# Attention with pooled keys and a gated convolution layer, one core: the order of a whole kernel's instructions from a new table, the first keys projected once, the last units gated on TensorE

## The chip, the cores and the metric

The kernel runs on one core of one Trainium2 chip. The metric is the device time of one execution in microseconds. The names of the engines in the profile: PE is TensorE (PEld its weight loads), DVE is VectorE, ACT is ScalarE, POOL is GpSimd, SP is SyncE, whose queue issues every DMA.

## The reference

```python
kv_pool = kv.reshape(B, H//4, 4, W//4, 4, C).mean(axis=(2, 4))      # B=4, 384x32 pixels, C=128
k = v = kv_pool.reshape(B, -1, C) @ w_sr                            # 768 keys per batch
s = (q @ k.transpose(0, 2, 1)) / sqrt(C)                            # 12288 queries per batch
a = exp(s - s.max(-1)); a /= a.sum(-1) + 1e-9
x = a @ v
gate = sigmoid(sum over 5 taps of conv_w[k] * x shifted by 4-k rows) # causal, per channel
out = (gate * (x @ w_val)) @ w_out
```

q is drawn 8 times and conv_w 200 times larger than in the plain layer, so the products keep float32's accuracy by splitting operands into a high and a low part.

## The kernel before, in words

The work is cut into groups of 512 queries (four tiles of 128), 24 groups per batch, 96 in all; the last group is two units of 256 (`LAST = (2, 2)`). A tile goes through these steps (`group`, L488):

- `score`: six matmuls into a PSUM tile `s` of 768 columns (high keys by high q, low keys by high q, high keys by low q). There are three `s` tiles.
- `row_max` (DVE, `nm`), `expo` (ACT), `unit_over_z` (two short DVE steps, `r`), then the high half `hl` (ACT, L579) and the low half (DVE, L590). Only this last DVE step gives the `s` tile back.
- `turn`: a transposing DMA of two tiles at once, `pt<-hl` (SP, L603). So a group needs two of them.
- 18 matmuls `av<-pt,vh` or `vl` (L674) once both are there, then `x` (ACT), the five-tap convolution on POOL (L731, L739; on DVE, L713 and L715, for the last three units, `TAIL`), `th` (tanh, ACT), `val` (PE, L756), `h` (DVE), `out` (PE, L765), `evac` (ACT, L770), and a store.

Per batch `setup` (L267) makes the keys and values: 16 pieces of kv are loaded (`kvt`, 384 KB each, L283), each is summed over 16 pixels (DVE, L305, in two halves; for some pieces of the first batch on POOL, L324), and the sums are projected by `w_sr` (PE, L359), split into `kh`, `kl` and `vt` (ACT L375, L387, DVE L399) and turned to values (L452 to L473). The first batch is set up before anything else can run; batches 2 to 4 are loaded two pieces at a time during the groups of the batch before, in eight blocks each, 20 us apart.

The order of all instructions is made by `Plan.order`: each step carries a duration, a due time from the table `DUE`, and the steps and buffers that it waits for; the planner walks through a model of the engines and takes on each the ready step with the earliest due time. The engines then run their lists strictly in that order. `WAIT`, `CLUMP` and `PERIOD` are weights of the same planner, `FIRST_Q` and `FIRST_VALS` its times for the first loads of q and the first values.

In the first batch the projection is cut by piece (17 parts, `project`, L346). `AGAIN = 3` issues each of the first 14 parts three times into the same place (L358); the repeats change no result. The eleven parts of the first 512 keys go to bank `m`, the rest to `av`:

```python
for _ in range(n):
    nc.tensor.matmul(steps[0].tile[:, c0 - lo:c1 - lo], wsr,
                     st["pool"][:, c0:c1], start=True, stop=True)
...
steps.append(part(c0, c1, AGAIN if first and c1 <= NK - 3 * PC else 1))
```

Of the kernel before, what the change touches and what calls it, by code (L numbers as in the profile page):

```python
# [22 lines left out]
PERIOD = 10.01  # L23
DUE = dict(keys=-40.3, vals=-31.67, vals0=8.05, q=-55.06, qh=7.59, ql=-74.93,
           score=(-7.35, -6.03, -4.51, -6.24), max=(-15.0, -3.7, 0.12, -12.81),
           exp=(5.62, -26.1, -4.96, -12.51), hi=(-28.69, -23.8, -4.13, -31.54),
           lo=(21.73, -24.19, 6.06, 6.76), turn=(-4.97, 24.57, 24.86, -0.88), pe=4.52, thi=58.42,
           tlo=9.94, r=(-46.22, -49.7, -33.31, -24.78), grid=-0.79, av=20.59, avs=4.62,
           halo=63.02, x=44.45, gate=28.59, th=59.85, val=49.41, h=2.48, out=18.96, evac=16.49,
           store=49.37)  # L30
# [11 lines left out]
class Plan:  # L42
# [5 lines left out]
    WAIT = dict(PE=0.08, ACT=0.3, DVE=0.1, POOL=0.01, SP=0.27)  # L48
    DMA_LEAD, DMA_TAIL, CLUMP = 1.3, 0.8, 24.47
# [99 lines left out]
def attn_moe_kernel(ctx, tc, qT, kvT, w_sr, w_moe, outT):  # L149
# [14 lines left out]
    D = DUE  # L164
# [67 lines left out]
    def weights():  # L232

        load_sr = plan.add("SP", 0.3, -20 * T - 35.5, lambda: nc.sync.dma_start(out=wsr, in_=w_sr))
# [32 lines left out]
    def setup(b, st):  # L267
# [7 lines left out]
        def load(i):  # L275
            buf = "o" if first and i in SPARE else "kvt"
            cuts = (0, PC * RR // 2, PC * RR) if first and i == PIECES - 1 else (0, PC * RR)

            def run(k):
                if k == 0:  # L280
                    steps[0].tile = tile_of(steps[0], buf)
                sl = slice(cuts[k], cuts[k + 1])
                nc.sync.dma_start(out=steps[0].tile[:, sl], in_=kvT[b, i, :, sl])  # L283
            steps = []
            for k in range(len(cuts) - 1):
                steps.append(plan.add(
                    "SP", (1.0 if first else 1.3) / (len(cuts) - 1),
                    due(-20 * T + i) if first else at(i), lambda k=k: run(k), steps[:],
                    takes=(buf,) if k == 0 else (), start=at(i)))
            return steps, buf  # L290
# [7 lines left out]
        def summed(i, ld, buf, part):  # L298
# [3 lines left out]
            def run():  # L302
                dst = pool_of(s, k0)[:, k0:k0 + n]
                src = ld[0].tile[:, :PC * RR].rearrange("c (k s) -> c k s", s=RR)
# [3 lines left out]
                         [ld[min(part, len(ld) - 1)], sums.get(0)], takes=("pool",) if k0 == 0 else (),  # L308
                         frees=[(ld[0], buf)], start=at(i))
# [542 lines left out]
```

## Time and profile before

| | |
|---|---|
| median of 3 runs | 1037.87 us (1037.05 to 1038.72) |
| the profiled execution | 1038.03 us, span 1036.2 us, so 1.83 us lie outside the span |
| PE busy | 1001.3 us, 97% of the span |
| DVE, POOL, ACT busy | 931.0, 928.8, 882.3 us (90%, 90%, 85%) |
| chain of waits | PE 81%, DMA 5%, DVE 4% |

The span runs from the first to the last instruction. A busy engine is one with an instruction in it, which for PE includes the repeated projections. The table of slices of the page shows PE below nine tenths in the first three slices only, and in the last.

### The profile page before, as it was taken

The page shows a single profiled execution, that of the slowest core. Times are in us where ns is not written, and L with a number is a line of the kernel's source. Part 1 is how long each engine was busy: PE and PEld are TensorE (multiplying, and loading weights), DVE is VectorE, ACT ScalarE, POOL GpSimd, SP SyncE. Part 2 cuts the span into 40 slices and gives each one's busy share as a digit, 9 for nine tenths or more (in the row PEclk, how much of TensorE's full clock was granted, in tenths as well). Part 3 has the DMA queues.
Part 4 walks back from the last instruction along what each step waited for, and adds up shares of the span by engine and source line. Part 5 has one row for each costly group of instructions (what it writes and reads, how often), then busy time and mean ns, then how long its engine had stood idle before and what let it go on. Part 6 is the DMA issues. An engine that isn't in the chain of part 4 may idle for free.

```text
span 1036.2 us, 15524 instructions
## 1 busy us (share of the span) xinstructions
PE 1001.3 (97%) x4600; PEld 618.6 (60%) x4600; DVE 931.0 (90%) x1810; ACT 882.3 (85%) x1575; POOL 928.8 (90%) x1067
## 2 busy tenths in 40 slices
PE   5779999999999999999999999999999999999997
PEld 5656655556665555566665565556666666666664
DVE  5699999999899999998989898999998898988985
ACT  0588998889898898899998898889999999889884
POOL 4159999999999998999999899899999999999994
PEclk9899999999999999999999999999999999999999
DMA  8399999999999999999999999999999999999983
GB/s 316 84 206 257 226 239 243 253 218 201 220 223 233 246 232 254 237 248 239 184 220 237 240 237 245 245 239 219 182 225 205 212 218 218 202 211 192 192 176 91
DMA packets 616851, 227.06 MB, mean 219 GB/s; under 512 B 595520, under 2 KB 596160, under 8 KB 616768
## 3 DMA queue, kind: packets, MB, share of 16 engines
q1 hardware_dynamic: 616768, 226.07, 101.1%
q8 instruction: 37, 0.61, 0.3%
q14 instruction: 46, 0.38, 0.1%
HBM read 50.66 MB, written 25.17 MB: 73 GB/s over the span
## 4 chain that ended last, share of the span: by engine, by line
PE 81%; DMA 5%; DVE 4%; ACT 1%; issue 1%; SPq 0%; ACTq 0%; DVEq 0%
PE s L532 34%; PE av L674 31%; PE m L765 7%; PE m L756 7%; DMA pt<-hl 3%; DMA kvt<-in_kv 2%; DVE hl L590 2%; DVE nm L544 1%; ACT hl L579 1%; DVE h L760 0%; PE m L452 0%; DVE pool L305 0%; PE m L359 0%; SPq L603 0%; ACT s L551 0%
## 5 line engine op out<-in xcount | busy, mean ns | idle before, releaser
L739 POOL TENSOR_TENSOR gate<-gate,tap 128x512 f32<-128x512 f32 x376 | 480.6, 1278 | 9.9
L590 DVE SCALAR_TENSOR_TENSOR hl<-s,r,hl 128x768 f16<-128x768 f32 x382 | 386.4, 1012 | 39.8 <-ACT hl L579 39.6
L674 PE MATMUL av<-pt,vh 128*128 128x512 f16 (+1 forms) x1164 | 384.3, 379 | 2.4 <-DMA pt<-hl 1.8
L551 ACT ACTIVATE s<-s,nm 128x768 f32<-128x768 f32 x384 | 336.4, 876 | 51.3 <-DVE nm L544 50.8
L544 DVE TENSOR_REDUCE nm<-s 128x1 f32<-128x768 f32 x384 | 362.5, 944 | 9.6 <-PE s L532 8.9
L579 ACT ACTIVATE hl<-s,r 128x768 f16<-128x768 f32 x382 | 338.4, 906 | 31.7 <-DVE r L565 24.0
L532 PE MATMUL s<-kh,qh 128*128 128x512 f32 (+1 forms) x768 | 265.7, 427 | 16.4 <-DVE hl L590 8.8
L731 POOL TENSOR_SCALAR tap<-x,wb 128x512 f32<-128x512 f32 x376 | 253.4, 693 | 0.0
L674 PE MATMUL av<-pt,vl 128*128 128x512 f16 (+1 forms) x582 | 219.6, 377 | 0.0
L532 PEld LDWEIGHTS s<-kh,qh 128*128 128x128 f32 x768 | 136.0, 191 | 128.5 <-issue 47.3
L674 PEld LDWEIGHTS <-vh 128*128 128x128 f16 x1164 | 112.3, 98 | 153.6 <-issue 56.4
L532 PE MATMUL s<-kl,qh 128*128 128x512 f32 (+1 forms) x768 | 199.9, 342 | 0.0
L532 PE MATMUL s<-kh,ql 128*128 128x512 f32 (+1 forms) x768 | 198.6, 340 | 0.0
L518 POOL TENSOR_TENSOR ql<-q,qh 128x512 fp32r<-128x512 f32 (+1 forms) x97 | 122.7, 1266 | 31.1 <-ACT qh L514 30.9
L532 PEld LDWEIGHTS s<-kl,qh 128*128 128x128 f32 x768 | 119.7, 191 | 17.5 <-DVE kl L399 0.2
L532 PEld LDWEIGHTS s<-kh,ql 128*128 128x128 f32 x768 | 119.4, 191 | 17.4
L731 POOL TENSOR_SCALAR gate<-x,wb 128x512 f32<-128x512 f32 x94 | 65.1, 693 | 42.2 <-ACT x L692 42.0
L765 PE MATMUL m<-h,wm 128*128 128x512 f32 x190 | 101.6, 616 | 0.6 <-DVE h L760 0.3
L756 PE MATMUL m<-x,wb 128*128 128x512 f32 x190 | 97.2, 593 | 0.7 <-ACT o L770 0.7
L674 PEld LDWEIGHTS <-vl 128*128 128x128 f16 x582 | 57.2, 98 | 62.3 <-issue 25.5
L770 ACT ACTIVATE o<-m 128x512 f32<-128x512 f32 x95 | 56.8, 597 | 23.0 <-PE m L765 22.4
L565 DVE RECIPROCAL r<-r 128x1 f32<-128x1 f32 x384 | 62.8, 164 | 13.1
(63 smaller groups left out, 628.3 us busy)
## 6 DMA issues: line engine op xcount, KB each, us to landing
q<-in_q SPq DMA_DIRECT2D x47, 512.0 KB, 4.7
out<-o SPq DMA_DIRECT2D x47, 512.0 KB, 3.4
kvt<-in_kv SPq DMA_DIRECT2D x60, 384.0 KB, 4.1
pt<-hl SPq DMA_TRANSPOSE x191, 5.8
o<-in_kv SPq DMA_DIRECT2D x3, 384.0 KB, 7.1
q<-in_q SPq DMA_DIRECT2D x2, 256.0 KB, 4.7
kvt<-in_kv SPq DMA_DIRECT2D x2, 192.0 KB, 4.5
raw<-in_w_moe SPq DMA_DIRECT2D x1, 261.0 KB, 2.8
```

What stands on the lines that cost most here:

```text
L518: nc.gpsimd.tensor_tensor(out=g.ql, in0=g.io.q[:, mine], in1=g.qh.bitcast(F32), op=ALU.subtract)
L532: nc.tensor.matmul(t[:, c0:c1], a[:, sl], k[:, c0:c1], start=(i == 0), stop=(i == 2))
L544: v.tensor_reduce(out=s.tile, in_=sc.tile[:, :NK], axis=AX.X, op=ALU.max, negate=True)
L551: nc.scalar.activation(out=sc.tile[:, :NK], in_=sc.tile[:, :NK], func=AF.Exp, bias=mx.tile, accum_out=sc.tile[:, NK:NK + 1])
L565: v.reciprocal(out=s.tile, in_=e.tile)
L579: nc.scalar.activation(out=g.hls[j // 2][:, half, 0], in_=sc.tile[:, :NK], func=AF.Copy, scale=r.tile)
L590: v.scalar_tensor_tensor(out=hl[:, half, 1], in0=sc.tile[:, :NK], scalar=r.tile, in1=hl[:, half, 0], op0=ALU.mult, op1=ALU.subtract)
L674: nc.tensor.matmul(g.av, st[name][:, k * P:(k + 1) * P], g.pt[:, :, a * NCH + k], start=(i == 0), stop=(i == len(AV) - 1))
L731: nc.gpsimd.tensor_scalar(out=s.tile, in0=src(k), scalar1=wt(k), scalar2=1.0, op0=ALU.mult, op1=ALU.mult)
L739: nc.gpsimd.tensor_tensor(out=g.gate, in0=g.gate, in1=tap.tile, op=ALU.add)
L756: nc.tensor.matmul(g.m, st["wb"][:, :C], g.x[:, HALO:], start=True, stop=True)
L765: nc.tensor.matmul(g.m2, wout, g.h, start=True, stop=True)
```

## The change

- `w_sr` is the first load on SP; it stood behind the fifth piece of kv.
- The first keys are projected once per piece (`AGAIN` is gone).
- The last piece's two half loads stand together in one step, and the first load of q behind them.
- The end is cut in units of 256, 128 and 128 queries in place of 256 and 256. The gate of the last two is made by PE: for each tap a diagonal matrix of its weights is made once (ACT, into the buffer `vt`, after the last batch's values), and five matmuls of x, shifted by one column each, sum the taps in PSUM. The last four units' `val` and `out` use `s` banks (`IN_S`); before, the last two did.
- A new table of due times and planner weights, so the whole program has a new order; separate due times for the last units.

```diff
-PERIOD = 10.01
-DUE = dict(keys=-40.3, vals=-31.67, vals0=8.05, q=-55.06, qh=7.59, ql=-74.93,
...
+PERIOD = 10.07
+DUE = dict(keys=-41.48, vals=-22.35, vals0=16.98, q=-57.56, qh=-1.25, ql=-98.01,
...
-    DMA_LEAD, DMA_TAIL, CLUMP = 1.3, 0.8, 24.47
+    DMA_LEAD, DMA_TAIL, CLUMP = 1.3, 0.8, 39.63
...
-        load_sr = plan.add("SP", 0.3, -20 * T - 35.5, lambda: nc.sync.dma_start(out=wsr, in_=w_sr))
+        load_sr = plan.add("SP", 0.2, -2000, lambda: nc.sync.dma_start(out=wsr, in_=w_sr))
...
-                        for _ in range(n):
-                            nc.tensor.matmul(steps[0].tile[:, c0 - lo:c1 - lo], wsr,
-                                             st["pool"][:, c0:c1], start=True, stop=True)
+                        nc.tensor.matmul(steps[0].tile[:, c0 - lo:c1 - lo], wsr,
+                                         st["pool"][:, c0:c1], start=True, stop=True)
...
-        if tail:
+        by_pe = g.i >= len(groups) - ON_PE
+        if by_pe:
+            gate, gate_by = taps_by_pe(g, w, n, held, late)
+        elif tail:
...
+        def diags(k):
+            def run():
+                if k == 0:
+                    s.tile = tile_of(s, "vt")
+                nc.scalar.activation(out=made[0].tile[:, k * C:(k + 1) * C], in_=ident, func=AF.Copy,
+                                     scale=st["wb"][:, C + k:C + k + 1])
...
+        def tap(k):
+            def run():
+                if k == 0:
+                    g.gate = tile_of(s, "s")[:, :w]
+                nc.tensor.matmul(g.gate, made[0].tile[:, k * C:(k + 1) * C], g.x[:, k:k + w],
+                                 start=(k == 0), stop=(k == TAPS - 1))
...
-TAIL, LAST, LAST_TURNED = 3, (2, 2), ((), (0, 1))
-AGAIN, FIRST_VALS = 3, 26.0
-FIRST_Q = {0: 15.0, 1: 19.0, 2: 22.0, 4: 26.0}
+ON_PE, IN_S = 2, 4
+TAIL, LAST, LAST_TURNED = 4, (2, 1, 1), ((), (0,), (0,))
+FIRST_VALS = 26.0
+FIRST_Q = {0: 17.0, 1: 17.5, 2: 18.0, 4: 26.0}
```

Three places of the new order. First the DVE where the first keys end (`kvt` is the last piece of kv, `kl` the low keys, `nm` the first row maximum). Before:

```order
L305 TENSOR_REDUCE pool_120<-kvt_165 128x24 x2
L305 TENSOR_REDUCE pool_120<-kvt_184 128x24
L399 SCALAR_TENSOR_TENSOR kl_227<-m_128,kh_213 128x512
L305 TENSOR_REDUCE pool_120<-kvt_184 128x24
L399 SCALAR_TENSOR_TENSOR kl_227<-av_209,kh_213 128x256
L544 TENSOR_REDUCE nm_265<-s_247 128x1
```

Now:

```order
L301 TENSOR_REDUCE pool_120<-kvt_155 128x24 x2
L301 TENSOR_REDUCE pool_120<-kvt_168 128x24 x2
L394 SCALAR_TENSOR_TENSOR kl_207<-m_127,kh_191 128x512
L394 SCALAR_TENSOR_TENSOR kl_207<-av_188,kh_191 128x256
L539 TENSOR_REDUCE nm_237<-s_219 128x1
```

The second half of the last piece was summed behind the low keys of the first 512; now both halves are summed before. On SP the load of q that stood between the two halves now follows them, and the fifth load of q stands ahead of the first transpose, as it did.

Second, SP in the third batch's loading (one block of 20 us: two pieces of kv, one load of q, one store, four transposes). Before:

```order
L603 DMA_TRANSPOSE pt_3970<-hl_3909 128x24x128
L283 DMA kvt_4039<-in_kv 128x768
L283 DMA kvt_4050<-in_kv 128x768
L603 DMA_TRANSPOSE pt_3970<-hl_3964 128x24x128
L603 DMA_TRANSPOSE pt_4099<-hl_4006 128x24x128
L504 DMA q_4125<-in_q 128x1024
L793 DMA out<-o_4025 128x1024
L603 DMA_TRANSPOSE pt_4099<-hl_4085 128x24x128
```

Now:

```order
L598 DMA_TRANSPOSE pt_4058<-hl_3974 128x24x128
L283 DMA kvt_4092<-in_kv 128x768
L283 DMA kvt_4096<-in_kv 128x768
L499 DMA q_4109<-in_q 128x1024
L598 DMA_TRANSPOSE pt_4058<-hl_4052 128x24x128
L598 DMA_TRANSPOSE pt_4172<-hl_4131 128x24x128
L794 DMA out<-o_3996 128x1024
L598 DMA_TRANSPOSE pt_4172<-hl_4185 128x24x128
```

The load of q moved up behind the two pieces. On DVE the first sum of the first of these pieces stood 25 places behind the low half that releases the transpose ahead of the loads; it now stands 15 places behind it in every other block and 19 in the blocks between. In the second batch's loading it stood 18 places behind and the block already had its q there; in the fourth's it stood 15 places behind in the last six blocks.

Third, the end of PE's list (`s<-x,vt` a tap, `wb` a `val`, `wm` an `out`). Before:

```order
L756 MATMUL s_12075<-x_12022,wb_8780 128x256
L756 MATMUL s_12080<-x_12047,wb_8780 128x256
L765 MATMUL m_12083<-h_12077,wm 128x512
L756 MATMUL m_12095<-x_11908,wb_8780 128x512
L765 MATMUL s_12100<-h_12097,wm 128x256
L765 MATMUL m_12106<-h_12102,wm 128x512
L765 MATMUL s_12114<-h_12111,wm 128x256
```

Now:

```order
L766 MATMUL s_12105<-h_12062,wm 128x512
L816 MATMUL s_12108<-x_12067,vt_8936 128x128
L766 MATMUL s_12112<-h_12102,wm 128x256
L816 MATMUL s_12108<-x_12067,vt_8936 128x128
L757 MATMUL s_12117<-x_12030,wb_8794 128x128
L816 MATMUL s_12108<-x_12067,vt_8936 128x128
L757 MATMUL s_12122<-x_12067,wb_8794 128x128
L816 MATMUL s_12108<-x_12067,vt_8936 128x128
L766 MATMUL s_12126<-h_12120,wm 128x128
L816 MATMUL s_12108<-x_12067,vt_8936 128x128
L766 MATMUL s_12136<-h_12133,wm 128x128
```

Both lists begin right behind the last `av`. One more `out` of 512 and the five taps of the unit before the last moved ahead of it, among the last `av` and the one before.

Outside these places, groups of 96 whose batch needs no loads have one and the same row of PE work in both orders (score, val, score, out, 3 av, score, 6 av, score, 9 av).

## Rows read from the trace of the kernel before

**Rows 1.** The page: busy time of each engine, and the chain of waits by engine.

```profile
PE 1001.3 (97%) x4600; PEld 618.6 (60%) x4600; DVE 931.0 (90%) x1810; ACT 882.3 (85%) x1575; POOL 928.8 (90%) x1067
PE 81%; DMA 5%; DVE 4%; ACT 1%; issue 1%; SPq 0%; ACTq 0%; DVEq 0%
```

**Rows 2.** Stretches (start and end, length, then busy us and instructions of PE, PEld, DVE, ACT, POOL, granted clock, DMA share, GB/s): three microseconds of the first loads, and two of 20 us.

```profile
15.00:18.00 3.00, 3.00 (x16) 3.00 (x16) 1.72 (x4) 0.00 (x0) 2.84 (x6) 1.00 1.03 399
...
60.00:80.00 20.00, 15.77 (x73) 10.45 (x70) 17.63 (x34) 15.49 (x29) 14.38 (x18) 0.91 1.06 212
...
760.00:780.00 20.00, 20.00 (x94) 12.35 (x93) 17.87 (x35) 18.10 (x33) 19.23 (x23) 1.00 1.09 231
```

**Rows 3.** The chain of waits in order of time (start us, us, what): the av that begins every second group, at both ends of the three loading stretches, and two neighbouring groups without loads.

```profile
81.25 2.61 PE av L674 x12
...
223.09 2.61 PE av L674 x12
...
315.40 2.82 PE av L674 x13
...
458.81 2.61 PE av L674 x12
...
551.15 2.82 PE av L674 x13
...
716.28 2.61 PE av L674 x12
...
808.51 1.31 PE av L674 x6
...
818.48 1.31 PE av L674 x6
```

**Rows 4.** The timeline of the first keys (start us, us, engine, line, operation, in brackets the idle time before and what ended it).

```profile
10.55 14.26 PE L359 MATMUL m<-pool,wsr 128*128 128x48 f32 x66 [10.55 <-DMA wsr<-in_w_sr]
...
17.23 0.42 SPq L283 DMA_DIRECT2D kvt<-in_kv  x1
...
20.82 0.26 POOL L324 TENSOR_TENSOR pool<-kvt 128x48 f32<-128x48 f32 x1
...
24.63 5.33 PE L359 MATMUL av<-pool,wsr 128*128 128x16 f32 x24
...
25.82 0.62 ACT L514 CAST qh<-q 128x512 fp32r<-128x512 f32 x1
...
26.52 1.26 POOL L518 TENSOR_TENSOR ql<-q,qh 128x512 fp32r<-128x512 f32 x1 [5.43 <-ACT qh L514]
26.58 0.54 DVE L305 TENSOR_REDUCE pool<-kvt 128x24 f32<-128x384 f32 x1
...
30.69 0.42 DVE L399 SCALAR_TENSOR_TENSOR kl<-av,kh 128x256 fp32r<-128x256 f32 x1 [3.57 <-ACT vt L387]
...
32.42 0.96 DVE L544 TENSOR_REDUCE nm<-s 128x1 f32<-128x768 f32 x1 [1.31 <-PE s L532]
```

**Rows 5.** The loads of the last piece's two halves (line 283 from 15 to 24 us), issue to landing.

```profile
DMA to landing us min/median/max: 4.4/4.5/4.7
```

**Rows 6.** The timeline from the first scores to the steady state: scores, the first transposes, the fourth low half, and two of PE's waits.

```profile
32.18 0.84 PE L532 MATMUL s<-kh,qh 128*128 128x512 f32 x2
...
34.10 0.84 PE L532 MATMUL s<-kh,qh 128*128 128x512 f32 x2
...
35.28 0.52 PE L532 MATMUL s<-kh,ql 128*128 128x512 f32 x2
...
38.98 0.98 PE L532 MATMUL s<-kh,qh 128*128 128x512 f32 x2 [3.18 <-DVE hl L590]
...
39.78 10.37 SPq L603 DMA_TRANSPOSE pt<-hl  x2
...
45.49 1.02 DVE L590 SCALAR_TENSOR_TENSOR hl<-s,r,hl 128x768 f16<-128x768 f32 x1 [0.32 <-ACT hl L579]
...
69.98 2.69 DVE L544 TENSOR_REDUCE nm<-s 128x1 f32<-128x768 f32 x3
...
75.65 0.60 PE L532 MATMUL s<-kh,qh 128*128 128x512 f32 x2 [3.32 <-DVE hl L590]
...
77.34 0.84 PE L532 MATMUL s<-kh,qh 128*128 128x512 f32 x2
```

**Rows 7.** DVE's timeline in the fourth batch's loading: the sums of a piece that waited longest for its load.

```profile
582.92 0.55 DVE L305 TENSOR_REDUCE pool<-kvt 128x24 f32<-128x384 f32 x1 [2.15 <-DMA kvt<-in_kv]
...
645.37 0.55 DVE L305 TENSOR_REDUCE pool<-kvt 128x24 f32<-128x384 f32 x1 [1.95 <-DMA kvt<-in_kv]
```

**Rows 8.** The chain of waits at the end (start us, us, what): a val and an out of 512 columns, and the last av.

```profile
1011.51 0.86 PE m L756 x2
...
1020.89 1.12 PE m L765 x2
...
1023.83 1.97 PE av L674 x18
```

**Rows 9.** The timeline of the end, and ahead of it six fp32 passes of 128 columns from the second batch's values, at full clock.

```profile
254.84 0.83 PE L452 MATMUL m<-diag,vt 128*128 128x128 f32 x6
...
1018.43 1.02 PE L756 MATMUL m<-x,wb 128*128 128x512 f32 x2
...
1024.00 0.10 PEld L674 LDWEIGHTS <-vl 128*128 128x128 f16 x1
...
1025.63 1.34 PE L756 MATMUL s<-x,wb 128*128 128x256 f32 x4
...
1032.92 0.33 SPq L787 DMA_DIRECT2D out<-o  x1
```

## What I expect, and how it is worked out

> **What bounds the kernel now.** I read the page first: PE is busy for 97% of the span and holds 81% of the chain of waits; DVE, POOL and ACT are at 85 to 90% [rows 1]. A share is a mean over stages, so the table by stretches comes next. In the steady state PE is busy for 20.00 of 20 us; between 60 and 80 us it is busy for 15.77, and DVE, at 17.63, is the fuller one [rows 2]. So there are a start, a steady state with loading stretches in it, and an end.
>
> The chain in order of time gives the period. Two neighbouring groups without loads begin 818.48 - 808.51 = 9.97 us apart; I use 9.98, or 19.96 for two [rows 3]. While the next batch is loaded two groups take longer: 223.09 - 81.25 = 141.84 for seven pairs, 2.1 more than 7 x 19.96; 458.81 - 315.40 = 143.41, 3.7 more; 716.28 - 551.15 = 165.13 for eight, 5.4 more [rows 3]. Together 11.2 us are lost there.
>
> I cost the change against the profiled execution, 1038.03 us; the median of the three runs is 0.16 less, and the last line is for the median.
>
> **Outside the three places.** A group without loads has the same PE list in both orders, and PE does not wait there: nothing. The five diagonals are short ACT steps, about 0.4 us each, spread over three groups in which ACT is busy for 18.1 of 20 us and PE for all 20 [rows 2]; PE's own work covers them, and without that cover they cost at most 2 us. Projections and values of batches 2 to 4 are the same instructions a few places earlier or later: nothing, and half a microsecond either way in the range. With `w_sr` in front the first loads move by one issue of 0.4 us; the later pieces stood behind it before too, so the last piece does not move by it.
>
> **The start.** The first 66 passes of the projection (33 issues, two passes each) run from 10.55 to 24.8 without a gap, 0.216 us each, and the next 24 to 29.96 [rows 4]. The sums that they need are there much earlier: POOL's last at 21.08, DVE's last could be there at 22.4 and is held by the low keys in front of it until 27.12. So PE, with its repeats, sets when the keys are there.
>
> Now there are 34 passes. The last half piece was issued at 17.23 [rows 4] and landed 4.5 us later [rows 5], at 21.8; without 256 KB of q ahead of it, 0.65 us at 399 GB/s [rows 2], it lands at 21.2. Its sum takes 0.54: 21.9. The last four parts of the projection, 0.43 each from POOL's 21.1 on, end at 22.9. High keys (0.4) and low keys (0.42) follow: 23.8. The cast of q (0.62) waits for a load that now stands behind all keys, about 22.0, so the low q (1.26) is ready at 24.0. The first score's last pair ends at 24.7, and the first row maximum, at 32.42 before [rows 4], stands at 24.8: **7.6 us earlier**.
>
> Does the clock take some of that back? In the old kernel PE has worked without a gap since 10.55 when the scores begin. Yet three pairs of score matmuls take 34.10 - 32.18 = 1.92 us and one shows 0.84, where at 35.28 one shows 0.52 [rows 6]: the first scores run at the half level of 1.2 GHz all the same. So the repeats did not buy speed there, and dropping them loses none. The Trainium skill, "TensorE: Matmul & The Clock Gate", part 1 on the clock gate, says that the clock is throttled by default and that sustained activity releases it, which speaks for such repeats; by it the third score too could stay slow, and the sum would be up by some 0.5 us.
>
> Then scores, maxima and low halves follow in nearly the same order as before. Three things differ. First, the second group's q is cast fourth, with three buffers for the high half: it waits for the end of the fourth score, 38.98 + 1.92 = 40.9 before [rows 6] and 33.3 now. Cast and low q take 1.9, and only then is a q buffer free for the fifth load, which stands ahead of the first transpose on SP. That one goes at 35.9 and not at 39.78 - 7.6 = 32.2 [rows 6]. The second transpose needs the fourth low half, which ended at 46.5 [rows 6]: 38.9 now, and 40 with one more maximum in front of it. That covers most of the delay; I take 1 us. Second, in the old order three maxima stood in a row at 69.98 with no low half between; PE waited 3.32 us for an `s` buffer at 75.65 and then ran at the half level again (0.84 at 77.34), about 1.7 us lost [rows 6]. The new order has no three in a row there, so part of these 5 us may go; but it has half an `av` less behind it by then (9 of 18 matmuls, 1.95 us). Third, one tile of the third group is scored ahead of the second group; its work is not lost. Together I take **-7.5**, with ends at -3.9 (the first transposes set the pace) and -10.5 (the gap goes).
>
> **The loading stretches.** DVE sums a piece at a fixed place of its list and waits there if the load is late; behind it stand the low halves that give `s` buffers back, and PE's scores wait for those. In the fourth batch's loading, with 15 places of DVE between the low half that releases the transpose ahead of the load and the first sum, such waits reach 2.15 and 1.95 us [rows 7]. The new order has 15 places in every other block of the loading stretches and 19 between. The 5.4 us of that stretch, over six blocks with 15 places, are 0.9 a tight block. Thirteen tight blocks at 0.9 and eleven looser ones at 0.13 give 13.2, **+2.0** against 11.2. For the range: -3 (a looser block lets the queue catch up) to +10 (every block like the tight ones).
>
> **The end.** From the `val` at 1018.43 to the span's end, 1036.2, are 17.8 us: the last `av` ends 7.2 after it, the last store is issued at 14.5, and 3.3 follow [rows 9]. In the new list more stands ahead of the end of the last `av`: two `val` (0.86 and 0.43), an `out` (0.86), five taps, and two `av` of 128 columns for one of 256 [rows 8]. A tap is two fp32 passes; six take 0.83 [rows 9], so 0.28 a tap. An `av` matmul of 256 columns takes 1.97 / 18 = 0.109 [rows 8]; one of 128 lies between half of that, 0.054, and the 0.10 of the weight load that goes with each [rows 9]; eighteen take 1.0 to 1.8. Down the list: `val` 0.86, twelve `av`, the `out` 2.46 after the start as before [rows 8], six `av`: 4.1. Then 0.86 + 0.86 + 0.43 + 0.86 + 5 x 0.28 and 36 small `av` (2.0 to 3.6): 10.5 to 12.1. Behind it two `out` (0.86, 0.43), five taps, two `val` and an `out` of 0.28 each: 3.5. Then tanh, h, out and evac of 128 columns, each with its hop, about 1.7, and the same 3.3. The sum is 19.0 to 20.6, or 1.2 to 2.8 more than 17.8. I take **+1.8**, nearer the upper end because a weight load goes with each matmul, and 0 to +3 for the range.
>
> The Trainium skill, same page, "Back-to-back issue gap", gives about 81 ns for a pair of load and matmul at 128 columns; by it the 36 take 2.9 and the term is 2.1.
>
> **Sum:** -7.5 + 2.0 + 1.8 = -3.7, so 1034.3 on the profiled execution and **1034.2 us** for the median. A change of 0.2%, 2.1 us, is about what a measurement of this kernel can tell from none.
>
> **Rivals.**
> 1. *The loading stretches take more than the start gives* (slower). If each of the 24 blocks costs the 0.9 us of the tight ones, 21.6 us are lost there and not 11.2: -7.5 + 10.4 + 1.8, 1042.6. It decides from 0.79 us a block on. For it: two waits of 2 us [rows 7], and DMA engines without slack (a share of 1.09 even without loads [rows 2]). Against it: four places more in every other block. Chance 0.13.
> 2. *The start is given back* (no change). If the first transposes set the pace, the start gains 39.78 - 35.9 = 3.9 and the time is 1037.8. For it: the load in front of them waits for three buffers. Against it: the second transpose is later anyway. Chance 0.22.
> 3. *The gap at 75 us goes too.* Then the start gives 10.5 and the time is 1031.2. For it: no three maxima in a row. Against it: DVE stays nearly full in that stretch [rows 2], so another wait may come. Chance 0.15.
>
> My forecast has the remaining 0.50.
>
> **How the numbers follow.** The likeliest case stands at 1034.2. The range 1028.5 to 1039.5 takes in cases 2 and 3 with the ends of the other terms and leaves out case 1. Faster: 0.15 and nearly all of 0.50, 0.63; within 0.2%: case 2 and a rest, 0.23; slower: 0.14.
>
> **What would show it.** Right: the first row maximum near 25 us; PE without waits from about 68; groups without loads still 9.98 apart; pairs in loading stretches near 20.5 in all three batches; a tail of 19 to 20.6 from the `val` behind the last full `av`. Wrong: a first maximum after 27, or a first `av` not 5 us earlier than before; load waits of 2 us in most blocks; a tail of 17.8 or less, which would mean that taps and small `av` cost nothing.

## The result and the profile after

| | before | after |
|---|---|---|
| median, six runs each | 1038.3 us (1036.31 to 1040.84) | 1046.82 us (1045.27 to 1049.91) |
| ratio, 95% interval | | 1.0082 [1.0062, 1.0103] |
| profiled execution | 1038.03 us, span 1036.2 | 1049.91 us, span 1048.0 |

The kernel became slower by 0.8%, where 1034.2 us was forecast. The profiled execution of after is the slowest of its six, 3.1 us above their median; the ledger below is of that execution.

The page, its busy time and its chain, against [rows 1]:

```profile
PE 1001.0 (96%) x4586; PEld 612.0 (58%) x4586; DVE 929.9 (89%) x1806; ACT 886.2 (85%) x1584; POOL 931.3 (89%) x1069
PE 82%; DMA 9%; DVE 6%; SPq 1%; issue 1%; ACT 1%; POOL 0%; ACTq 0%
```

No engine has more to do; PE has as many busy us in a span 11.8 longer. DMA has gone from 5 to 9% of the chain. So something waits for transfers, and the next question is where.

The chain in order of time gives the place. These are the starts of the `av` that stand where the first, third, fourth and seventh of [rows 3] stood (81.25, 315.40, 458.81, 808.51):

```profile
74.25 2.82 PE av L669 x13
...
314.47 2.82 PE av L669 x13
...
466.99 2.61 PE av L669 x12
...
820.11 1.31 PE av L669 x6
```

They moved by -7.0, -0.9, +8.2 and +11.6, and the span's end by +11.8. So the start gave 7.0, the three loading stretches took 6.1, 9.1 and 3.4, together 18.6, and from there to the end the two kernels differ by 0.2.

**The start**, against [rows 4] and the 20 us of [rows 2]:

```profile
25.74 0.96 DVE L539 TENSOR_REDUCE nm<-s 128x1 f32<-128x768 f32 x1 [1.31 <-PE s L527]
```

```profile
60.00:80.00 20.00, 17.93 (x88) 11.09 (x88) 19.20 (x38) 17.45 (x32) 17.14 (x20) 1.00 1.13 227
400.00:420.00 20.00, 17.79 (x74) 10.14 (x72) 15.58 (x31) 15.02 (x27) 16.09 (x19) 0.91 1.13 242
...
760.00:780.00 20.00, 19.98 (x99) 13.13 (x98) 17.92 (x38) 19.05 (x37) 17.85 (x22) 1.00 1.11 214
```

The first row maximum stands 6.7 us earlier. Between 60 and 80 us PE is busy for 17.93 where it was 15.77: the gap of 3.32 at 75.65 of [rows 6] is gone. Without loads, between 760 and 780, PE is full as before. In the middle row, in the third batch's loading, PE is not full, DVE less still, and the granted clock is down.

**A loading block.** The waits of DVE and of PE (total us, times, longest):

```profile
DVE hl L585 <- ACT hl L574: 37.5, 113, 1.6
DVE pool L301 <- DMA kvt<-in_kv: 21.8, 16, 2.7
DVE nm L539 <- PE s L527: 13.9, 27, 1.8
```

```profile
PE s L527 <- DVE r L555: 17.2, 13, 2.4
PE s L527 <- DVE hl L585: 8.7, 8, 3.2
PEld m L766 <- DVE h L761: 7.6, 36, 0.4
```

(The last is the wait of PE's weight load for `h`; it comes in again with e9.) DVE's wait for a piece and PE's for an `s` tile behind `r` were, before:

```profile
DVE pool L305 <- DMA kvt<-in_kv: 11.0, 12, 2.2
...
PE s L532 <- DVE r L560: 7.5, 7, 2.4
```

How they hang together is seen in one block: SP's queue, DVE and PE (the timeline, idle time in brackets), and one piece of the chain of waits:

```profile
129.24 3.68 SPq L598 DMA_TRANSPOSE pt<-hl  x1
132.98 1.07 SPq L283 DMA_DIRECT2D kvt<-in_kv  x2
134.15 0.38 SPq L499 DMA_DIRECT2D q<-in_q  x1
134.62 6.23 SPq L598 DMA_TRANSPOSE pt<-hl  x1
140.95 0.53 SPq L794 DMA_DIRECT2D out<-o  x1
141.58 4.61 SPq L598 DMA_TRANSPOSE pt<-hl  x1
...
133.93 1.02 DVE L585 SCALAR_TENSOR_TENSOR hl<-s,r,hl 128x768 f16<-128x768 f32 x1
137.34 0.55 DVE L301 TENSOR_REDUCE pool<-kvt 128x24 f32<-128x384 f32 x1 [2.38 <-DMA kvt<-in_kv]
137.80 1.01 DVE L585 SCALAR_TENSOR_TENSOR hl<-s,r,hl 128x768 f16<-128x768 f32 x1
138.73 0.15 DVE L555 SCALAR_TENSOR_TENSOR r<-s,unit 128x1 f32<-128x1 f32 x1
...
138.96 0.59 PE L527 MATMUL s<-kh,qh 128*128 128x512 f32 x2 [2.11 <-DVE r L555]
...
140.79 1.06 PE L669 MATMUL av<-pt,vh 128*128 128x512 f16 x2
```

```profile
132.98 4.33 DMA kvt<-in_kv
```

The load goes at 132.98, when the transpose in front of it lets SP go, and lands at 137.3. DVE came to the sum at 134.95 and stands for 2.38 us; the low half and the `1/Z` behind it are late by as much, and PE stands for 2.11. The two loads, the load of q and a transpose of 6.23 us fill SP until 140.9, so the store and the transposes behind them go later too; PE's own waits for transposed data are only 3.1 us in all. The last line of the timeline shows a second loss: two `av` take 1.06 us where 0.59 is the measure at full clock. The table by stretches has it in four places, each at the end of such a wait of PE (2.11 to 2.44 us):

```profile
139.80:143.20 3.40, 3.40 (x10) 1.29 (x10) 2.92 (x8) 2.73 (x6) 1.97 (x2) 0.50 1.20 304
412.80:416.20 3.40, 3.40 (x11) 1.78 (x11) 2.70 (x6) 2.25 (x4) 2.27 (x2) 0.50 1.39 214
457.20:460.60 3.40, 3.40 (x10) 1.48 (x9) 2.98 (x7) 2.57 (x6) 1.92 (x2) 0.50 1.25 217
665.40:668.80 3.40, 3.18 (x9) 2.06 (x10) 2.50 (x7) 1.75 (x3) 1.75 (x2) 0.50 1.13 271
```

Granted clock 0.50, the 1.2 GHz level, for 3.4 us: half of that, 1.7 us of work, is lost each time, some 6.8 of the 18.6. In the loading stretches of before there is no such place.

Not every block is like this one. In the third batch's loading the chain has these `av`, each of the second group behind the one above:

```profile
398.93 2.82 PE av L669 x13
...
422.98 2.61 PE av L669 x12
...
443.01 2.82 PE av L669 x13
...
466.99 2.61 PE av L669 x12
```

Two groups take 24.05, 20.03 and 23.98 us, where 19.96 is the pace without loads. The first and the last of these pairs hold a block with 15 places on DVE between the low half and the first sum, where DVE waits 2.47 and 2.37 us for the load; the middle one holds a block with 19 places and no such wait. Over the whole trace DVE waits 19.0 us for kv outside the start: 16.5 of it in the nine blocks with 15 places, 0.4 in the nine with 19, the rest in the six others.

### The profile page after: what moved, and what is told of

It is laid out like the page before. It is cut to its first block, busy times and chain, and to the rows that moved or that the text cites. A ratio compares the mean times of both kernels' runs of the same rounds, so it can differ in the third digit from the quotient of the medians.

```text
span 1048.0 us, 15461 instructions
## 1 busy us (share of the span) xinstructions
PE 1001.0 (96%) x4586; PEld 612.0 (58%) x4586; DVE 929.9 (89%) x1806; ACT 886.2 (85%) x1584; POOL 931.3 (89%) x1069
## 4 chain that ended last, share of the span: by engine, by line
PE 82%; DMA 9%; DVE 6%; SPq 1%; issue 1%; ACT 1%; POOL 0%; ACTq 0%
PE s L527 35%; PE av L669 31%; PE m L757 7%; PE m L766 7%; DMA kvt<-in_kv 4%; DMA pt<-hl 4%; DVE hl L585 3%; DVE nm L539 2%; DVE pool L301 1%; DMA o<-in_kv 1%; SPq L598 1%; ACT hl L574 0%; PE m L354 0%; SPq L283 0%; PE m L447 0%
## 5 line engine op out<-in xcount | busy, mean ns | idle before, releaser
L669 PE MATMUL av<-pt,vh 128*128 128x512 f16 (+2 forms) x1176 | 385.8, 379 | 3.1 <-DMA pt<-hl 3.1
L539 DVE TENSOR_REDUCE nm<-s 128x1 f32<-128x768 f32 x384 | 362.8, 946 | 14.4 <-PE s L527 13.9
L527 PE MATMUL s<-kh,qh 128*128 128x512 f32 (+1 forms) x768 | 267.5, 429 | 26.2 <-DVE r L555 17.2
L669 PE MATMUL av<-pt,vl 128*128 128x512 f16 (+2 forms) x588 | 222.2, 378 | 0.0
L527 PEld LDWEIGHTS s<-kl,qh 128*128 128x128 f32 x768 | 119.6, 191 | 17.6 <-DVE kl L394 0.2
L301 DVE TENSOR_REDUCE pool<-kvt 128x24 f32<-128x384 f32 x114 | 60.4, 540 | 21.8 <-DMA kvt<-in_kv 21.8
L771 ACT ACTIVATE o<-m 128x512 f32<-128x512 f32 x94 | 56.3, 599 | 23.0 <-PE m L766 22.3
```

Of the source, the lines that this page charges most:

```text
L301: v.tensor_reduce(out=dst, in_=src[:, part * n:][:, :n], axis=AX.X, op=ALU.add)
L527: nc.tensor.matmul(t[:, c0:c1], a[:, sl], k[:, c0:c1], start=(i == 0), stop=(i == 2))
L539: v.tensor_reduce(out=s.tile, in_=sc.tile[:, :NK], axis=AX.X, op=ALU.max, negate=True)
L669: nc.tensor.matmul(g.av, st[name][:, k * P:(k + 1) * P], g.pt[:, :, a * NCH + k], start=(i == 0), stop=(i == len(AV) - 1))
```

## The experiments

My theory at first: the new table puts loads on SP too late for the places of their sums on DVE; every other part of the loss follows from that wait. The rivals: the new code (no repeats, the cut end) is the loss; SP has too many changes between copies and transposes in a block; the DMA engines are full, and the order doesn't matter; or the sums' own place on DVE is wrong and not SP's.

For all kernels I give one measure beside the time: the **loss in the three loading stretches**, which is the time between the starts of the 2nd, 22nd, 45th and 69th `out` on PE, less 9.975 us for each of the 20, 23 and 24 groups between. About 3.4 of each is the matmuls of the next batch's keys and values and no wait (the smallest seen). Then come three waits of the whole execution: DVE's for a piece of kv (2.8 of it lie in the start wherever it is lowest), PE's for an `s` tile behind `r`, and PE's for transposed data. Loss and waits are of one profiled execution each; the medians are of 4 to 10 runs (after and before 6). The ratio is to runs of before made beside each kernel, whose median lay between 1038.3 and 1040.62 us, so where two rows stand close the ratios tell more than the times. In e1 to e7 the planner made the lists of all engines anew; from e8 on every list is that of the kernel from which the run starts, but for the one list that is named.

| kernel | median us | ratio to before [95%] | loss in the stretches | DVE for kv | PE for r | PE for pt |
|---|---|---|---|---|---|---|
| before | 1038.3 | 1 | 5.9, 6.3, 8.1 | 11.0 | 7.5 | 1.8 |
| after | 1046.82 | 1.0082 [1.0062, 1.0103] | 12.2, 15.8, 11.1 | 21.8 | 17.2 | 3.1 |
| e1 | 1034.49 | 0.9949 [0.9930, 0.9969] | 6.2, 9.1, 6.6 | 14.2 | 12.5 | 0.8 |
| e2 | 1044.19 | 1.0050 [1.0031, 1.0069] | 11.3, 11.0, 12.0 | 22.1 | 15.4 | 0 |
| e3 | 1050.2 | 1.0102 [1.0064, 1.0140] | 11.4, 10.9, 14.8 | 30.4 | 22.0 | 0.2 |
| e4 | 1052.45 | 1.0117 [1.0095, 1.0139] | 8.8, 15.2, 11.7 | 26.7 | 17.6 | 0.3 |
| e5 | 1037.94 | 0.9984 [0.9971, 0.9997] | 20.3, 3.7, 7.2 | 6.5 | 3.7 | 4.3 |
| e6 | 1043.98 | 1.0038 [1.0020, 1.0056] | 24.2, 3.9, 9.1 | 12.4 | 5.2 | 2.7 |
| e7 | 1048.27 | 1.0077 [1.0049, 1.0105] | 11.2, 9.0, 10.2 | 14.4 | 9.7 | 5.8 |
| e8 | 1033.67 | 0.9935 [0.9912, 0.9958] | 9.1, 9.5, 7.0 | 16.2 | 10.2 | 2.2 |
| e9 | 1042.97 | 1.0026 [1.0004, 1.0048] | 9.5, 12.8, 9.3 | 2.8 | 1.3 | 5.5 |
| e10 | 1050.21 | 1.0081 [1.0063, 1.0099] | 12.7, 12.6, 12.5 | 2.8 | 4.3 | 0.5 |
| e11 | 1039.74 | 0.9982 [0.9972, 0.9992] | 8.8, 9.5, 7.4 | 2.9 | 2.8 | 0.5 |
| e12 | 1043.55 | 1.0029 [1.0009, 1.0049] | 7.4, 11.0, 7.8 | 2.8 | 3.8 | 2.4 |
| e13 | 1046.06 | 1.0071 [1.0044, 1.0097] | 8.8, 13.2, 11.4 | 22.3 | 19.9 | 0 |
| e14 | 1023.19 | 0.9849 [0.9824, 0.9875] | 4.5, 3.4, 5.1 | 2.8 | 4.9 | 0 |
| e15 | 1021.88 | 0.9838 [0.9810, 0.9865] | 4.5, 3.4, 3.4 | 2.8 | 5.0 | 0.3 |
| e16 | 1032.89 | 0.9919 [0.9891, 0.9946] | 5.4, 9.3, 4.8 | 2.8 | 4.6 | 8.2 |
| e17 | 1043.33 | 1.0029 [1.0002, 1.0057] | 4.7, 11.8, 6.9 | 2.8 | 2.4 | 10.2 |
| e18 | 1026.31 | 0.9877 [0.9830, 0.9925] | 6.8, 4.2, 4.7 | 2.8 | 3.0 | 4.2 |

### The code or the table (e1, e7)

e1 is the new code with the old table; e7 the old code with the new table.

```diff
-PERIOD = 10.07
+PERIOD = 10.01
-DUE = dict(keys=-41.48, ... grid=-0.27, ... store=61.44, ...)
+DUE = dict(keys=-40.3, ... grid=-0.79, ... store=49.37, ...)
-    WAIT = dict(PE=0.08, ACT=0.2, DVE=0.11, POOL=0.01, SP=0.59)
-    DMA_LEAD, DMA_TAIL, CLUMP = 1.3, 0.8, 39.63
+    WAIT = dict(PE=0.08, ACT=0.3, DVE=0.1, POOL=0.01, SP=0.27)
+    DMA_LEAD, DMA_TAIL, CLUMP = 1.3, 0.8, 24.47
```

Expected of e1: 

> The changed kernel with the old table of dues, the old period, waits and clump (the tail's dues are the old ones); first keys, order of the first loads, diagonals and end stay new. If the loss comes from the table: start -7.5 and end +0.4 to +1.8 against before and the loading stretches as before, 1031 to 1034 us, PE loses under 9 us in waits in all. If it comes from the new structure (an earlier start that meets the loads at another phase): 1042 to 1047.

Expected of e7: 

> The kernel before with the new table of dues, period, waits and clump alone; the old first keys, first loads and end. If the table is the loss wherever the start lies: 1046 to 1054, its third batch's loading (same order on SP and the same 15 and 19 places as in the changed kernel) some 8 us longer than with the old table. If the loss needs the earlier start, that stretch is as before, 1038 to 1042.

The new code alone is faster than before by 0.5% (1034.49), and the new table alone is as slow as the whole change (1048.27 against 1046.82). The table is the loss, with either code. e1 stands on the forecast's number, for a kernel that is not the one forecast.

### How the copies stand in a block of SP (e2, e3, e4)

In e2 the store's due time moves by two groups, so that it stands with the loads; in e3 q and store come one group later, so that there are two groups of copies; in e4 q alone, which makes three.

```diff
-           store=61.44, ...                                    # e2
+           store=81.58, ...
-  at = FIRST_Q[g.i] if ... else grid(t0 + D["q"])             # e3, e4
+  at = FIRST_Q[g.i] if ... else grid(t0 + D["q"]) + (0 if g.i < 6 else T)
-  at = grid(t0 + D["store"])                                  # e3
+  at = grid(t0 + D["store"]) + T
```

Expected of e2: 

> The changed kernel with the store due two groups later, so that SP issues it behind the loads and q, in one clump per block, and four transposes follow without a copy between; DVE's places are 15 in nearly every block. Theory A (SP's queue paces the loading stretches, and each change from copies to transposes costs the transpose behind it 1 us or more): a block falls from 21.4 to about 20.6, 22 blocks give 13 to 18 us, 1030 to 1035. Theory B (the piece sum stands too early on DVE and waits there for its load; the low halves behind it wait): 15 places in every block instead of every other one, so the waits of 2 us double, 1047 to 1057.

Expected of e3: 

> The changed kernel with q and the store put one group later than the loads: two clumps of copies per block (loads, two transposes, q and store, two transposes), as the old kernel had in its third batch; DVE's places are 15 in every block. Theory A: as many changes from copies to transposes as the new table's, but smaller clumps, so its first transposes wait less; blocks of 20.5 to 21, 1033 to 1041. Theory B: 1047 to 1057, as with the store in the clump.

Expected of e4: 

> The changed kernel with only q put one group later than the loads: three clumps of copies per block (loads; store; q). DVE's places are 15 in every block. Theory A: one more change from copies to transposes than the two-clump form, 0.5 to 1 us a block more: 10 to 20 us above the two-clump kernel. Theory B: no difference from the two-clump kernel, 1047 to 1057.

e2 is 2.6 us under after and e3 and e4 are 3.4 and 5.6 above it, with more waits for kv, not fewer (22.1, 30.4, 26.7). The time does rise with the changes from copies to transposes in a block (one in e2, two in after and e3, three in e4). But e2, with the fewest, still loses 34.3 us in the stretches where before loses 20.3, so their number doesn't explain the loss.

### All dues of the grid earlier (e5, e6)

```diff
-  grid=-0.27
+  grid=-2.77     # e5; -3.07 in e6
```

Expected of e5: 

> The changed kernel with one number of the new table altered: the loads' grid 2.5 us earlier. In the third and fourth batch's loading every block is then loads, q, two transposes, store, two transposes, as with the old table, and 20 places of DVE stand between the low half that releases the transpose ahead of the loads and the first piece sum, instead of 15 and 19 in turn. Theory B (DVE has almost no slack in these stretches, and what it waits for a load is lost): waits for pieces fall from 21.8 us to under 5, each of the two stretches from 152 and 149 us to about 141, 1024 to 1031 in all. Theory A (SP's queue and the DMA engines set the pace there): the same bytes and the same number of copy groups, so blocks stay at 20.5 to 21.5, 1036 to 1045.

Expected of e6: 

> The same with 2.8 us: SP's order stays as with 2.5 in the third and fourth batch's loading, but DVE's places are 20 in the third and 15 in the fourth batch's. Theory B: the third batch's stretch as with 2.5, and the fourth's some 4 to 6 us longer than that, with waits of about 1 us a block. Theory A: both stretches alike.

With e5 the second and third stretches lose 3.7 and 7.2 us and not 15.8 and 11.1, and DVE waits 6.5 us for kv. The first stretch loses 20.3, though that is partly the measure's beginning: its 2nd `out` stands 6.8 us earlier than in after and its 22nd 1.3 later. The planner puts every list anew for such a number, so it is no clean test; 0.3 us more (e6) costs 6 us. It shows that another plan can be without most of the loss in a stretch, and leaves open whether that is the loads' doing.

### Half the bytes (e8)

```diff
-  for c0, c1 in zip(cuts, cuts[1:]):
+  for c0, c1 in zip(cuts, cuts[1:] if first else (PC * RR // 2,)):
...
-  v.tensor_reduce(out=dst, in_=src[:, part * n:][:, :n], axis=AX.X, op=ALU.add)
+  v.tensor_reduce(out=dst, in_=src[:, (part if first else 0) * n:][:, :n], ...)
```

Expected of e8: 

> The changed kernel with half of each kv piece of batches 2 to 4 left out: a load moves 192 KB and both sums read the half that came. Every instruction stays at its place. Theory B: a landing takes 1 us less or more, the waits for pieces fall under 6 us, 1028 to 1036. If the new order of DVE, ACT and PE costs by itself, without late loads: no change, 1043 to 1047.

1033.67, 13.2 us under after, with lists that are otherwise the same. Half as many bytes land in 3.1 us (median) in place of 4.3, and 5.6 us of waits for kv go; 16.2 stay, where I had expected under 6. The four places at half clock, 6.8 us, are gone too. The size of the transfer matters, so this alone does not tell late loads from full DMA engines; e14, with every byte in place, does.

### The sums later on DVE (e9 to e12)

Every sum of batches 2 to 4 is moved behind the next four steps of DVE's list (e9; nine in e10; four with the old table in e11 and in the kernel before in e12). All other lists are the same.

```diff
+            s.late = not first
...
-    for step in plan.order():
+    for step in later(plan.order(), 4):
```

Expected of e9: 

> The changed kernel with every piece sum of batches 2 to 4 moved four places down DVE's list, behind the next four instructions of DVE; the lists of SP, PE, ACT and POOL are word for word the same. That makes 19 to 20 places before the first sum of the tight blocks and 23 to 24 of the others. Theory B (DVE waits for the load at the place of the sum, the low halves behind it wait, and PE waits for those): waits for pieces fall from 21.8 us to under 6, and of the 39 us that the three stretches lose 17 to 25 come back: 1021 to 1031. If SP's queue and the DMA engines set the pace: no more than 3 us, 1043 to 1047.

Expected of e10: 

> The same with nine places, 24 to 29. Theory B: as with four places to within 3 us, since the waits are gone with four; what is left then is DVE's own work in these stretches and PE's. If each place more is worth something by itself: clearly faster than four places.

Expected of e11: 

> The changed kernel with the old table, and the piece sums of batches 2 to 4 four places later. Theory B: waits for pieces fall from 14.2 us to under 5, and the 22 us that the three stretches lose to 12 to 15: 1024 to 1029. Otherwise 1033 to 1036 as with the old table alone.

Expected of e12: 

> The kernel before with the piece sums of batches 2 to 4 four places later, nothing else. Its waits for pieces in those stretches are some 9 us, most in the fourth batch's (15 places). Theory B: 4 to 8 us faster than before, 1031 to 1035. Otherwise no change.

Here my theory in its first form fell. The wait at the sums is gone in all four (2.8 us, the start's), yet little comes back: e9 gains 3.9 us against after (5.8 by the ratios), e10 has after's ratio (1.0081 and 1.0082), and e11 and e12 are slower than the kernels that they change, e11 by 3.4 us by the ratios (0.9982 for 0.9949) and e12 by 2.9 against the runs beside it (1.0029 [1.0009, 1.0049]). e9's waits show what came in their place:

```profile
DVE hl L599 <- ACT hl L588: 43.7, 131, 1.1
DVE nm L553 <- PE s L541: 24.4, 49, 3.0
...
DVE pool L314 <- DMA kvt<-in_kv: 2.8, 3, 0.9
```

```profile
PEld m L780 <- DVE h L775: 18.0, 65, 0.6
...
PE av L683 <- DMA pt<-hl: 5.5, 5, 2.3
...
PE s L541 <- DVE r L569: 1.3, 1, 1.3
```

DVE waits 10.5 us more for scores and 6.2 more for ACT's high halves, and PE 2.4 more for transposed data. That last wait is not what the four have in common: it is 0.5 in e10 and in e11. What is higher in all four is PE's wait for `h` ahead of `out`, here that of its weight load: 18.0, 17.7, 20.3 and 20.9 us in e9 to e12, where it is 7.6 in after, 8.7 in e1 and 9.0 in before. So the sums at their later places hold up other steps of DVE that PE needs. How much of the time each of these waits costs is not taken apart here, as a weight load's wait is partly covered by matmuls.

### The loads earlier on SP (e13, e14, e15, e16, e17, e18)

Now SP's list alone is changed, behind the planner: the two loads and the q beside them pass the one transpose ahead of them (e14); the store that stands one transpose behind them passes the next (e13); both (e15). e16 and e17 are the same code with the old table and in the kernel before, e18 is two transposes in place of one. In e16 and e17 the load of q does not move along in most blocks of the third and fourth batch's loading, so that there the two loads move alone.

```diff
+    placed = plan.order()
+    sp = [s for s in placed if s.eng == "SP"]
+    for k, s in enumerate(sp[1:], 1):
+        if s.kind == "load" and sp[k - 1].kind == "turn":
+            n = 1
+            move(placed, s, -1)
+            while sp[k + n].kind in ("load", "query"):
+                move(placed, sp[k + n], -1)
+                n += 1
-    for step in plan.order():
+    for step in placed:
```

Expected of e13: 

> The changed kernel with one move in SP's list alone: where the store stands behind the first transpose after the loads and q, it goes behind the second, so that every block of the loading stretches is loads, q, two transposes, store, two transposes, as with the old table. The lists of PE, DVE, ACT and POOL are word for word the same. If the store's place is the cause: the transpose behind it takes 3.8 us instead of 4.6, half of the blocks lose 1 us less, and the waits of PE and DVE with them: 1034 to 1040. If the loads stand too late for DVE's sums and nothing else counts: 1044 to 1048.

Expected of e14: 

> The changed kernel with the two loads and q of every block of the loading stretches one transpose earlier in SP's list; the other lists are the same, DVE's sums stand where they did. 25 to 29 places instead of 15 to 19. If late loads are the cause (and the sums moved later lost again by making DVE's other work late): waits for pieces gone, transposes on time, 1026 to 1034. If SP's transposes pace the blocks: each transpose that the loads now pass comes 1.6 us later and waits longer behind the copies, PE waits for it: 1043 to 1052.

Expected of e15: 

> Both moves of SP's list together: the store behind the third transpose, the loads one transpose earlier. If both count and add up: some 3 to 6 us below the better one. If only the loads count: as with the loads alone to within 2 us.

Expected of e16: 

> The changed kernel with the old table and the loads of batches 2 to 4 one transpose earlier in SP's list (q does not move in most blocks, so it stands alone behind a transpose: one more change from copies to transposes per block). If late loads are worth their waits of 14 us: 1024 to 1030. If the extra change costs a transpose 1 us per block: 1034 to 1045.

Expected of e17: 

> The kernel before with the loads of batches 2 to 4 one transpose earlier in SP's list, the other lists unchanged. If what the move gave the changed kernel (23 us) comes from waits for pieces, the kernel before has 9 us of them to give back, most in the fourth batch's loading: 1031 to 1036. If it comes from the move itself, whatever waits there are: 1015 to 1025.

Expected of e18: 

> The changed kernel with the loads and q two transposes earlier in SP's list. One transpose earlier no wait for a piece was left, so a second should give nothing: 1020 to 1026. If earlier is better by itself: 1010 to 1018. If the loads now stand ahead of transposes that are due: PE waits for those, 1028 to 1045.

e14 is at 1023.19 us: 23.6 under after and 15.1 under before (16.9 against the runs beside it, 0.9849 [0.9824, 0.9875]). One transpose on one queue is worth more than the whole loss. The same block as above, SP and then the same sum (the 35th) on DVE:

```profile
120.77 4.35 SPq L622 DMA_TRANSPOSE pt<-hl  x1
125.17 1.06 SPq L306 DMA_DIRECT2D kvt<-in_kv  x2
126.33 0.38 SPq L522 DMA_DIRECT2D q<-in_q  x1
126.82 10.30 SPq L622 DMA_TRANSPOSE pt<-hl  x2
...
133.18 0.54 DVE L324 TENSOR_REDUCE pool<-kvt 128x24 f32<-128x384 f32 x1
```

The load goes 8.0 us ahead of its sum, where in after DVE came to it 2.0 us behind the load's issue, and the sum has no wait beside it. PE's wait for transposed data is 0, and the half clock is gone from the stretches. With the store moved too (e15) the stretches are as full as the steady state, at full clock. The whole stretch of the third batch's loading, between the 22nd and the 45th `out`, first in after and then in e15:

```profile
302.00:547.00 245.00, 237.19 (x1075) 142.06 (x1074) 221.40 (x432) 211.11 (x376) 223.89 (x254) 0.99 1.08 224
```

```profile
293.00:526.00 233.00, 232.97 (x1077) 141.16 (x1075) 221.56 (x433) 211.48 (x377) 224.25 (x254) 1.00 1.12 234
```

The same work of every engine in 12 us less, and PE without a gap. The DMA engines carry 234 GB/s in place of 224 and a share of 1.12 in place of 1.08: they can do more than they did in after, so they were not the bound. So with the sums where they stand, the late loads on SP are the loss. The steps between a late load and PE are shown for the block above, not for every block. The store's move alone does nothing that the intervals can tell (e13), nor does it on top of e14. Two transposes (e18) are no better than one: PE's wait for transposed data, 0 in e14, is 4.2 us.

In the kernel before the move gives nothing (e17, 1.0029 [1.0002, 1.0057]), where I had expected 1031 to 1036. Its waits for kv fall to the start's 2.8, and in their place:

```profile
PE av L699 <- DMA pt<-hl: 10.2, 8, 2.3
```

That was 1.8. Of the 10.2 us 6.5 lie in the third batch's loading and 3.7 in the fourth's. With the old table in the new code (e16) the same wait is 8.2. So the place of the loads is a balance between the sums on DVE and the transposes for PE, and the new table had room for the transposes that it did not use. Why the old table has less room, and what the load of q that stayed behind adds, is not shown. e15 beats both kernels: 1021.88 us, 1.6% under before.

## Why the prediction was wrong, step by step

**The start (-7.5 forecast, -7.0 measured) held in its size, and only in part in its working.** The first row maximum came at 25.74 (24.8 forecast, under the mark of 27). PE's repeats bought nothing for the scores: the third goes at full pace without them, at 27.30, a pair of its matmuls in 0.52 as in [rows 6]. The term that the Trainium skill's "TensorE: Matmul & The Clock Gate", part 1, offered for a third slow score did not come. But the first `av` stands 5.3 us earlier (54.04 to 48.72), not 6.6, which was 7.6 less the 1 put for the second transpose. The fifth load of q, which was to hold up the first transpose until 35.9, was issued at 27.10, and the first two transposes go at 32.56; they take 13.35 us for the 10.37 of [rows 6], and the granted clock is at its 1.2 GHz level from 30.5 to 44.2, where in before it was from 38.5 to 42.0 and from 45.4 to 48.8 (whether the repeats had to do with that is not shown):

```profile
30.50:44.20 13.70, 10.05 (x30) 7.84 (x31) 9.20 (x21) 9.09 (x17) 1.28 (x1) 0.50 0.32 71
```

Against that the gap at 75 us went, as rival 3 said it could, and 1.7 us were gained between the first `av` and the one at 74.25, where about 0.9 was put. So two misses of about a microsecond partly cancelled, which is luck. Rival 3's time, 10.5 us earlier, did not come, and rival 2's, 3.9 earlier, is out as well.

**The loading stretches (+2.0 forecast, +18.6 measured) are the step that failed: the price of a tight block.** I priced a block by the number of DVE places between a low half and the first sum, 0.9 us where there are 15 and 0.13 where there are 19. The split between the two held, as the waits of 16.5 and 0.4 us and the pair of 20.03 us above show. The size did not. The loss is 39.1 us by the experiments' measure against 20.3, of which 3 x 3.4 are work in both; the 28.9 that remain are 1.2 us a block over all 24, where before had 0.42, and 2.4 for each of the twelve with 14 or 15 places if these bear it all. The pairs of 24.05 and 23.98 us are 4.1 and 4.0 above the pace.

Two things were wrong in the price. A place is no time: the loads go when the transposes ahead of them on SP are done, and not when the low half is. In the six blocks of the old list that the price was taken from, DVE came to the sum 1.4 to 3.6 us after the load's issue, in four of them over 3; in the nine blocks of the new list with as many places it came 0.8 to 2.7 us after it, and these loads took 3.4 to 4.3 us to land. And the waits cost more than in the old list. There 5.6 us of waits in the fourth batch's loading stood beside 5.4 us lost; here 19.0 stand beside 28.9, of which 6.8 are the four places at half clock.

Rival 1, which I had at 0.13, has the right sign and the nearest time, 1042.6, but not the working: it had all 24 blocks cost the 0.9 of the tight ones. Its counterargument, four places more in every other block, was true and did not help, as the tight blocks alone cost more than it put on all. The mark "load waits of 2 us in most blocks" did not come: there are 13 waits in 24 blocks outside the start, five of them of 2 us or more, the longest 2.7. The mark of pairs near 20.5 in all three batches failed at 24.05.

Since the profiled execution lies 3.1 above its median, about 15.5 of the 18.6 belong to the median if all of that lies in the stretches: -7.0 + 15.5 + 0.2 is 8.7, and the medians differ by 8.5.

**The end (+1.8 forecast, nothing measured).** From the `val` behind the last full `av` to the span's end are 1048.0 - 1030.20 = 17.8 us, exactly those of before. "A tail of 17.8 or less" was the mark, but it does not mean here what I wrote beside it, that taps and small `av` cost nothing. Two terms were too high, as this timeline shows:

```profile
1036.21 0.22 PE L669 MATMUL av<-pt,vl 128*128 128x128 f16 x1
1036.27 0.28 PE L669 MATMUL av<-pt,vh 128*128 128x128 f16 x2
1036.38 0.22 PE L669 MATMUL av<-pt,vl 128*128 128x128 f16 x1
...
1038.65 0.44 PE L816 MATMUL s<-x,vt 128*128 128x128 f32 x2
1038.93 0.22 PE L669 MATMUL av<-pt,vh 128*128 128x128 f16 x1
...
1044.08 1.73 SPq L788 DMA_DIRECT2D out<-o  x2
```

Three `av` of 128 columns take 0.17, 0.055 each, so the 36 take 2.0 and the lower end of my range was right: the weight load of 0.10 [rows 9] that goes with each adds nothing to it. The 81 ns that the Trainium skill gives for such a pair ("TensorE: Matmul & The Clock Gate", "Back-to-back issue gap") are not seen here; its 56 ns for a matmul alone are. A tap cost its 0.28. The last store was issued at 1045.5, 15.3 behind the `val` where it was 14.5, and the span ends 2.5 later, where I had put the 3.3 of a large store. Up to the last store the sum was 1.0 too high, of which the small `av` are some 0.6, and behind it 0.8: together the 1.8.

**Outside the three places** nothing was lost, as put: PE is full there (19.98 of 20) and groups are 9.97 to 9.98 apart.

The step behind all this: the forecast took the loss of six blocks of the old list, and the waits in two of them [rows 7], as a price for a new list whose SP order was also new. What was to be read was when SP issues each load against when DVE comes to its sum, in the old list too.

## What to carry to other kernels

When an engine waits for a load at a fixed place of its list, look at what stands in front of that load on the queue that issues it: here moving two loads and a q past one transpose gave 23.6 us, while moving the waiting instruction back gave 3.9, as it then held up other instructions of its own engine. Count the time between the issue and the instruction that needs the load, not the places in a list. A wait of 2 us in front of a full engine can cost more than 2 us, as the instructions behind it feed others; price the chain and not the wait. Take such a move one step at a time, and look at the other user of the queue: in the kernel before nearly the same move only changed which engine waited.

## What the runs showed of the hardware that I had not expected

- A transposing DMA takes longer on SP's queue when plain copies stand before it: 3.68 us behind another transpose, 4.61 behind a store, 6.23 behind two loads and a q, in the block shown, with the transposes' inputs done before they began. Over the whole execution the medians are 3.66 (101 transposes), 4.58 (45), and 5.76 behind any load of q (45).
- The granted clock falls to the 1.2 GHz level for 3.4 us at the end of single waits of PE of 2.11 to 2.44 us in an otherwise full stretch, at four places; a fifth wait, of 1.91 us, was not followed by it. Without these waits (e15) it stays at 1.00 through the same stretches.
- The first two scores run at half pace, 0.64 us from one pair of matmuls to the next against 0.35 later, before and after. The trace's first record of the granted clock is its step to full, at 27.1 us in after and 35.1 in before, and the pace changes just there; the column of the stretches shows 1.00 ahead of it (23.7 to 27), so it tells nothing of the time before the first record. In before PE had worked without a gap since 10.55 [rows 4] when the step came; in after, with 1.58 of 3 us busy between 15 and 18, it came 8 us earlier.
